# A fixed deviation bound, proved at the end, and pair differences from one fp16 half on two 32-row products

## The chip, the cores and the metric

The kernel runs on one core of a Trainium2 chip. The time is device microseconds of one execution of the whole kernel, as the median of several runs. One execution was taken with the hardware profiler; its trace gives the start and length of each instruction on TensorE (PE, with PEld for its weight loads), VectorE (DVE), ScalarE (ACT), GpSimd (POOL) and SyncE (SP, which issues the DMAs).

## The reference

There are 4 batches of 12480 tokens with 128 channels, 32 inducing points, and an MLP of 2048 hidden units with a squared ReLU.

```python
def mab(q, kv):
    s = scale * (q @ kv.transpose(0, 2, 1))
    a = softmax(s)                      # over the last axis, +1e-09 in the sum
    return a @ kv
h = mab(I, x)                           # per batch: 32 rows of 128
attn = mab(x, h)                        # per token: 32 weights, then a @ h
r = np.maximum(attn @ w_in, 0.0)        # 2048 columns
out = (r * r) @ w_out                   # 128 columns
```

## The kernel before

A token's attention output is a mix of the 32 rows of h with weights a that lie close to 1/32. So the kernel writes a = 1/32 + d and multiplies h into w_in once per batch. A hidden column whose 32 values all have one sign under every possible d needs no ReLU: it is either dead or plainly squared. The squares of all plain columns together are a quadratic form in d, with 512 coefficients: 16 x 31 pair differences and 16 further rows. Columns of mixed sign are few (at most 16 are allowed) and are computed one by one. A bound rho on the deviation says which column is which.

For each batch b the program has four parts:

- `first(b)` (L240): scores of 7 groups G of tokens (`scores`, L234, four fp32 products side by side on 32 columns each), their exponentials, and h by `hacc` (L323). Inside it `largest(G)` (L290) takes, on DVE, the largest magnitude of each row of the group's x, 128 x 1920 values.
- `prepare(b)` (L437): h times w_in (`hwv`, L448), the bound rho from the largest x and the spread of h (L454 to L459, L474 to L485), the sorting of the columns (L499 to L513), and from these the weights `w16` (L605 to L613), `lin`, `osc` and `bias` of the quadratic form.
- `second(b, G)` (L349): the token scores against h, their softmax, and d = a - 1/32, scaled by 2^14, as an upper and a lower fp16 half (L385 to L388). Both go to DRAM (L389) and come back transposed by `load_dT` (L404): rows 0 to 31 of `dT` are the upper half, 32 to 63 the lower, 64 to 95 the upper again. `squares` (L414) fills rows 96 to 127 with the mixed columns.
- `Chunk` (L629), 26 of 480 tokens in each batch: `up(j)` for j = 0, 1 makes two products of `pairs` with dT into two PSUM banks (`hp`, L639); `lift(j)` squares both on ACT in one instruction (L648); `down()` multiplies by w16 (four products, L654) and lin (one, L655) and brings the result out with scale and bias on ACT (L658) or DVE (L660), and SP stores it (L661).

`up` gives its product 96 rows. The matrix `pairs` (L106 to L114) holds one difference of unit vectors per column, once on rows 0 to 31 and again on 32 to 63, so that upper and lower half are added.

The order of the work is written out in the loop at L739: lift, the next chunk's up, the chunk before's down, then `background` (L721), which gives out pieces of `second`, `squares`, and the next batch's `first` and `prepare` by fixed counts. A scheduler with its own estimates of instruction lengths then orders each engine's queue; instructions whose inputs are early can be put far ahead. `hp` has two buffers, so `up` waits for the `lift` of the chunk before. Where an operation can run on ACT or DVE, `to_act` (L152) compares the sums in `held`, to which the program adds what it gives each engine; `largest` adds about 2 us to DVE's each time (L291). At the end the flags of all batches (the bound was small enough, few enough mixed columns, sizes fit) pick whether the general path `every_column` has to run (L899); in these runs it does not.

Of the kernel before, what the change touches and what calls it, by code (L numbers as in the profile page):

```python
# [9 lines left out]
F32 = mybir.dt.float32  # L10
# [20 lines left out]
MX = 16  # L31
RHO_MAX = 2.0 ** -8
NX = 9
# [7 lines left out]
def attend_then_relu2_mlp(ctx: ExitStack, tc: tile.TileContext, xn, xT, indT, w_in, w_out, outT):  # L41
# [65 lines left out]
    nc.vector.memset(pairs, 0.0)  # L107
    fold_f = fold.rearrange("p k i -> p (k i)")
    for s in range(1, 17):
        n = MI if s < 16 else 16  # L110
        nc.vector.tensor_tensor(
            pairs[0:64, MI * (s - 1):MI * (s - 1) + n], fold_f[0:64, 0:n], fold_f[0:64, s:s + n], op=ALU.subtract,
        )
    nc.vector.tensor_copy(pairs[0:64, 31 * 16:32 * 16], fold_f[0:64, 0:16])  # L114

# [3 lines left out]
    inv_t = const.tile([P, 1], F32, name="inv_t")  # L119
    flags = const.tile([1, NB], F32, name="flags")  # L120

# [4 lines left out]
    for k in range(2):  # L126
        one = Batch()
        one.xm = const.tile([P, NG], F32, name=f"xm{k}")
# [111 lines left out]
    def first(b):  # L240
# [48 lines left out]

        def largest(G):  # L290
            held["dve"] += 60 + 1.042 * 4 * WID[G]  # L291
            nc.vector.tensor_reduce(  # L292
                st.xm[:, G:G + 1], st.xp[G], axis=AX.X, op=ALU.max, apply_absolute_value=True,
            )

        def exp(G):
# [10 lines left out]
        for G, nb32 in enumerate(BLK):  # L307
# [5 lines left out]
            if G + 2 < NG:  # L313
                exp(G + 2)
            largest(G)
            yield
# [32 lines left out]
    def second(b, G, again=False):  # L349
# [39 lines left out]
        nc.sync.dma_start(st.ad[:, :, :, 480 * G:480 * G + w].rearrange("q i h n -> (q i) h n"), a16[:, :, 0:w])  # L389
        if not again:  # L390
            st.aT[G] = load_dT(b, G)
        yield
# [44 lines left out]
    def prepare(b):  # L437
# [6 lines left out]
        for h in range(2):  # L444
            ps = att_psum(f"hwv_{b}_{h}")
            for k in range(8):
                f = (8 * h + k) * P
                nc.tensor.matmul(  # L448
                    ps[:, k * (MI + 1):(k + 1) * (MI + 1)], w_in_sb[:, f:f + P], st.hT[:, 96:P + 1], start=True, stop=True,
                )  # L450
            evac(hwv[:, 8 * h:8 * h + 8].rearrange("p k i -> p (k i)"), ps[:, 0:8 * (MI + 1)], 8 * (MI + 1))
            if h == 0:

                xm, dh, ah = small("xm"), small("dh", MI), small("ah", MI)  # L454
                nc.vector.tensor_reduce(xm, st.xm, axis=AX.X, op=ALU.max)
                ts(dh, st.hT[:, 0:MI], st.hT[:, P:P + 1], None, op0=ALU.subtract)
                stt(dh, dh, -1.0, dh, op0=ALU.mult, op1=ALU.max)
                stt(ah, st.hT[:, 0:MI], -1.0, st.hT[:, 0:MI], op0=ALU.mult, op1=ALU.max)
                stt(dh, ah, 2.0 ** -18, dh, op0=ALU.mult, op1=ALU.add)  # L459
            yield  # L460
# [12 lines left out]
        nc.tensor.transpose(ps[0:1, 0:P], am, ident)  # L473
        nc.tensor.matmul(ps[0:1, P:P + MI], xm, dh, start=True, stop=True)  # L474
        row = work.tile([1, 2], F32, tag="row", name=f"row_{b}")
        nc.vector.tensor_reduce(row[:, 0:1], ps[0:1, 0:P], axis=AX.X, op=ALU.max)
        nc.vector.tensor_reduce(row[:, 1:2], ps[0:1, P:P + MI], axis=AX.X, op=ALU.max)
        ts(row[:, 0:1], row[:, 0:1], 2.0 ** -60, None, op0=ALU.max)
        ts(row[:, 1:2], row[:, 1:2], 2 * scale * (1 + 2.0 ** -8), 2.0 ** -16, op0=ALU.mult, op1=ALU.add)
        yield  # L480
        ps = att_psum(f"bc_{b}")
        nc.tensor.matmul(ps[:, 0:2], ones, row, start=True, stop=True)
        two = small("two", 2)
        nc.vector.tensor_copy(two, ps[:, 0:2])
        rho = two[:, 1:2]  # L485
        p2 = small("p2")
        ts(p2.bitcast(I32), two[:, 0:1].bitcast(I32), 0x7F800000, None, op0=ALU.bitwise_and)
        mg, nmg, s, k2, omr = small("mg"), small("nmg"), small("s"), small("k2"), small("omr")
        ts(k2, p2, 2.0, None, op0=ALU.mult)
# [10 lines left out]
        ts(nmg, p2, -2.0 ** -16, None, op0=ALU.mult)  # L500
        ts(omr, rho, -1.0, 1.0, op0=ALU.mult, op1=ALU.add)
# [7 lines left out]
        ts(dn, lo, 0.0, rho, op0=ALU.min, op1=ALU.mult)  # L509
        tt(dn, dn, vm, op=ALU.add)  # L510
# [34 lines left out]
        stt(inc, inc, pl, mix, op0=ALU.add, op1=ALU.mult)  # L545
        fits = work.tile([1, 2], F32, tag="fits", name=f"fits_{b}")
        ts(fits[:, 0:1], bp[0:1, 2:3], MX + 0.5, None, op0=ALU.is_le)
        ts(fits[:, 1:2], row[:, 1:2], RHO_MAX, None, op0=ALU.is_le)
        tt(flags[:, b:b + 1], fits[:, 0:1], fits[:, 1:2], op=ALU.mult)

# [78 lines left out]
    class Chunk:  # L629
# [73 lines left out]
    N_SECOND, N_SCORES, N_HEADS, N_PRE, N_SQ = 4, 2 * NG, 20, 23, 2  # L703
    ahead = chain(*(second(b, G) for b in range(NB) for G in range(NG)))
    sqs = chain(*(squares(b, G) for b in range(NB) for G in range(NG)))
# [15 lines left out]
    def background(k):  # L721

        b, c = k // (2 * NCH), k % (2 * NCH) / 2.0
        give("ahead", ahead, min(math.ceil((NG * b + c / 4 + min(3, 2 + k / 16)) * N_SECOND), NB * NG * N_SECOND))
        if b + 1 < NB:
# [214 lines left out]
```

## Time and profile before

| | us |
|---|---|
| median of 3 runs | 576.62 (575.87 to 576.66) |
| profiled execution, first to last instruction | 577.3 |
| PE busy | 438.9 |
| DVE busy | 365.3 |
| ACT busy | 296.8 |
| POOL busy | 83.4 |

The profiled execution's span is the whole time that the trace shows of it; it lies 0.7 us above the median. A busy PE is not a PE at its peak: the length of a matmul in the trace contains the way through the array, and consecutive ones overlap. So the distance from start to start is what counts there.

### The profile page before, as it was taken

The page shows a single profiled execution, that of the slowest core. Times are in us where ns is not written, and L with a number is a line of the kernel's source. Part 1 is how long each engine was busy: PE and PEld are TensorE (multiplying, and loading weights), DVE is VectorE, ACT ScalarE, POOL GpSimd, SP SyncE. Part 2 cuts the span into 40 slices and gives each one's busy share as a digit, 9 for nine tenths or more (in the row PEclk, how much of TensorE's full clock was granted, in tenths as well). Part 3 has the DMA queues.
Part 4 walks back from the last instruction along what each step waited for, and adds up shares of the span by engine and source line. Part 5 has one row for each costly group of instructions (what it writes and reads, how often), then busy time and mean ns, then how long its engine had stood idle before and what let it go on. Part 6 is the DMA issues. An engine that isn't in the chain of part 4 may idle for free.

```text
span 577.3 us, 8820 instructions
## 1 busy us (share of the span) xinstructions
PE 438.9 (76%) x3083; PEld 204.5 (35%) x3083; DVE 365.3 (63%) x947; ACT 296.8 (51%) x419; POOL 83.4 (14%) x93
## 2 busy tenths in 40 slices
PE   1615465777798889769878899769777999897882
PEld 0014334522233536413333545313243555223330
DVE  6999758662555268997254298985534378767342
ACT  0030112437577266747875376628574476565771
POOL 0000011030211010242021021222011022422010
PEclk9999655997789569989889799969969599899997
DMA  8958715024528606565867535735866332334543
GB/s 322 399 214 277 277 69 154 1 86 155 179 80 305 199 20 226 172 182 167 280 226 230 178 102 186 270 104 145 311 211 190 107 105 72 97 126 130 168 132 131
DMA packets 64590, 100.82 MB, mean 175 GB/s; under 512 B 22800, under 2 KB 53776, under 8 KB 64528
## 3 DMA queue, kind: packets, MB, share of 16 engines
q1 hardware_dynamic: 64528, 100.08, 52.1%
q8 instruction: 28, 0.46, 0.3%
q14 instruction: 34, 0.28, 0.2%
HBM read 64.91 MB, written 31.95 MB: 168 GB/s over the span
## 4 chain that ended last, share of the span: by engine, by line
PE 44%; DVE 28%; ACT 13%; issue 6%; DMA 3%; POOL 3%; SPq 1%; POOLq 0%; ACTq 0%; DVEq 0%
PE po L654 10%; PE hp L639 9%; ACT g L648 8%; PE s L236 7%; DVE xm L292 5%; PE hwv L448 5%; PE hacc L323 4%; DVE G L605 3%; DMA outT_dram<-o 2%; PE po L655 2%; PE wq L611 2%; ACT o L658 2%; DVE e L362 2%; PE R L529 2%; DVE z L372 2%
## 5 line engine op out<-in xcount | busy, mean ns | idle before, releaser
L648 ACT ACTIVATE g<-hp 128x960 f16<-128x960 f32 x208 | 193.2, 970 | 87.9 <-PE hp L639 48.9
L639 PE MATMUL hp<-dT,pairs 96*128 96x480 f16 x416 | 122.0, 385 | 29.0 <-ACT g L648 28.1
L654 PE MATMUL po<-g,w 128*128 128x480 f16 x416 | 119.4, 399 | 16.1 <-ACT o L658 6.0
L368 POOL TENSOR_TENSOR e<-e,mx 128x480 f32<-128x480 f32 (+1 forms) x28 | 26.5, 947 | 334.8 <-DVE mx L364 222.8
L639 PEld LDWEIGHTS <-pairs 96*128 96x128 f16 x416 | 37.8, 99 | 97.6 <-issue 75.7
L654 PEld LDWEIGHTS <-w 128*128 128x128 f16 x416 | 41.1, 104 | 75.4 <-issue 43.9
L292 DVE TENSOR_REDUCE xm<-xp_False 128x1 f32<-128x1920 f32 (+1 forms) x28 | 55.7, 1989 | 5.3 <-DMA xp_False<-xT_dram 5.3
L658 ACT ACTIVATE o<-po,bias,osc 128x480 f32<-128x480 f32 x66 | 48.9, 753 | 18.9 <-PE po L655 7.1
L236 PE MATMUL s<-xp_False,indT_sb 128*32 128x480 f32 (+1 forms) x224 | 37.7, 743 | 20.5 <-DMA xp_False<-xT_dram 12.3
L323 PE MATMUL hacc<-xnb,en 128*32 128x128 f32 x784 | 39.2, 328 | 17.2 <-issue 9.3
L655 PE MATMUL po<-dT,lin 128*128 128x480 f16 x104 | 42.3, 408 | 2.7 <-DMA dT<-zz 2.7
L432 POOL TENSOR_TENSOR zz<-z 128x480 f16<-128x480 f32 (+1 forms) x28 | 28.9, 1030 | 87.8 <-DVE z L428 72.1
L660 DVE TENSOR_SCALAR o<-po,osc,bias 128x480 f32<-128x480 f32 x38 | 28.7, 767 | 18.0 <-DMA outT_dram<-o 6.8
L323 PEld LDWEIGHTS hacc<-xnb,en 128*32 128x32 f32 x784 | 26.7, 129 | 34.3 <-issue 20.1
L300 ACT ACTIVATE sT<-sT,nb 128x480 f32<-128x480 f32 (+1 forms) x28 | 18.2, 653 | 35.5 <-DVE nb L287 35.5
L236 PE MATMUL s<-xp_False,hT 128*32 128x480 f32 (+1 forms) x224 | 34.5, 628 | 2.1 <-DVE s L357 1.7
L375 POOL TENSOR_TENSOR e<-e,z 128x480 f32<-128x480 f32 (+1 forms) x28 | 27.6, 986 | 53.8 <-DVE z L374 48.6
L428 DVE TENSOR_SCALAR z<-sq,off,cut 128x480 f32<-128x480 f32 (+1 forms) x28 | 21.4, 764 | 21.8 <-PE sq L422 21.7
L605 DVE TENSOR_TENSOR G<-hwp,hw 128x512 f16<-128x512 f16 x64 | 30.1, 510 | 5.0 <-PE wq L611 4.7
L369 ACT ACTIVATE e<-e 128x480 f32<-128x480 f32 (+1 forms) x28 | 16.1, 574 | 31.6 <-POOL e L368 31.6
L362 DVE STREAM_TRANSPOSE e<-s 128x480 f32<-128x480 f32 (+1 forms) x28 | 18.0, 644 | 15.4 <-PE s L236 14.9
L331 DVE TENSOR_TENSOR hq<-hacc,hq 128x128 f32<-128x128 f32 x24 | 6.8, 284 | 33.0 <-PE hacc L323 33.0
(208 smaller groups left out, 498.6 us busy)
## 6 DMA issues: line engine op xcount, KB each, us to landing
outT_dram<-o SPq DMA_DIRECT2D x104, 240.0 KB, 2.2
xp_False<-xT_dram SPq DMA_DIRECT2D x24, 960.0 KB, 5.8
xnb<-xn_dram SPq DMA_DIRECT2D x28, 448.0 KB, 6.1
xnb<-xn_dram SPq DMA_DIRECT2D x24, 512.0 KB, 5.8
dT<-ad SPq DMA_DIRECT2D x72, 120.0 KB, 2.7
ad<-a SPq DMA_DIRECT2D x24, 240.0 KB, 2.7
dT<-zz SPq DMA_DIRECT2D x104, 30.0 KB, 1.9
wi<-w_in_dram SPq DMA_DIRECT2D x4, 512.0 KB, 5.4
```

Source lines behind the costliest of these rows:

```text
L236: nc.tensor.matmul(ps[32 * q:32 * q + 32, 0:w], lhsT, xp[:, w * q:w * q + w], start=True, stop=True,)
L292: nc.vector.tensor_reduce(st.xm[:, G:G + 1], st.xp[G], axis=AX.X, op=ALU.max, apply_absolute_value=True,)
L323: st.last = nc.tensor.matmul(hacc[32 * q:32 * q + 32, 0:P], en[:, t], xg[:, t % 8], start=t < 4, stop=t + 4 >= nb32,)
L362: nc.vector.transpose(ef[:, 0:wb], ps[:, 0:wb])
L432: nc.gpsimd.tensor_tensor(g[rows], zv[rows], zv[rows], op=ALU.mult)
L448: nc.tensor.matmul(ps[:, k * (MI + 1):(k + 1) * (MI + 1)], w_in_sb[:, f:f + P], st.hT[:, 96:P + 1], start=True, stop=True,)
L605: tt(g[:, :, MI * j:MI * j + n], hwp[:, :, 0:n], hw16f[:, :, s0:s0 + n], op=ALU.mult)
L639: nc.tensor.matmul(hp[:, i, 0:CH].rearrange("p (q t) -> p q t", q=4), pairs[0:96, (2 * j + i) * P:(2 * j + i + 1) * P], self.dT[0:96], sta ...
L648: nc.scalar.activation(self.g[:, 2 * j:2 * j + 2], self.hp.pop(j)[:, 0:2, 0:CH], AF.Square)
L654: nc.tensor.matmul(po[:, 0:CH], st.w16[:, i], self.g[:, i], start=i == 0, stop=False)
L655: nc.tensor.matmul(po[:, 0:CH].rearrange("p (q t) -> p q t", q=4), st.lin, self.dT, start=False, stop=True)
L658: nc.scalar.activation(o, po[:, 0:CH], AF.Identity, bias=st.bias, scale=st.osc)
```

## The change

- `largest` and everything that made rho from data goes: the 28 reductions over x, the spread of h, one small product, and the second column of `row`, `two` and `fits`. rho is the constant 2^-10.
- `second` gains one DVE instruction for each group: the elementwise minimum of the upper half of d with a running minimum `least_d` (128 x 480 fp16). After the last group `smallest()` reduces it, and one more flag says whether every d was at least -0.498, which is what rho = 2^-10 asks for.
- `pairs` has each difference once: for products with even number on rows 0 to 31, for odd ones on rows 64 to 95. `up(j)` multiplies the first product with rows 0 to 31 of dT and the second with rows 64 to 95, so each has 32 rows, and the lower half of d (rows 32 to 63) is not used there. `squares` and `lin` read dT as before.

```diff
-RHO_MAX = 2.0 ** -8
+RHO = 2.0 ** -10
+D_MIN = -0.498
...
+    def half_rows(block):
+        return slice(64, 96) if block % 2 else slice(0, 32)
+
     for s in range(1, 17):
         n = MI if s < 16 else 16
+        r = half_rows((s - 1) // 4)
         nc.vector.tensor_tensor(
-            pairs[0:64, MI * (s - 1):MI * (s - 1) + n], fold_f[0:64, 0:n], fold_f[0:64, s:s + n], op=ALU.subtract,
+            pairs[r, MI * (s - 1):MI * (s - 1) + n], fold_f[r, 0:n], fold_f[r, s:s + n], op=ALU.subtract,
         )
...
+    least_d = const.tile([P, CH], F16, name="least_d")
+    nc.vector.memset(least_d, 0.0)
...
-        def largest(G):
-            held["dve"] += 60 + 1.042 * 4 * WID[G]
-            nc.vector.tensor_reduce(
-                st.xm[:, G:G + 1], st.xp[G], axis=AX.X, op=ALU.max, apply_absolute_value=True,
-            )
...
-            largest(G)
...
         if not again:
+            nc.vector.tensor_tensor(least_d[:, 0:w], least_d[:, 0:w], a16[:, 0, 0:w], op=ALU.min)
             st.aT[G] = load_dT(b, G)
...
-            if h == 0:
-
-                xm, dh, ah = small("xm"), small("dh", MI), small("ah", MI)
-                nc.vector.tensor_reduce(xm, st.xm, axis=AX.X, op=ALU.max)
...
-        nc.tensor.matmul(ps[0:1, P:P + MI], xm, dh, start=True, stop=True)
...
-        ts(vm, v, omr, None, op0=ALU.mult)
-        ts(up, hi, 0.0, rho, op0=ALU.max, op1=ALU.mult)
+        ts(vm, v, 1.0 - RHO, None, op0=ALU.mult)
+        ts(up, hi, 0.0, RHO, op0=ALU.max, op1=ALU.mult)
...
             for i in range(2):
+                r = half_rows(i)
                 nc.tensor.matmul(
-                    hp[:, i, 0:CH].rearrange("p (q t) -> p q t", q=4), pairs[0:96, (2 * j + i) * P:(2 * j + i + 1) * P],
-                    self.dT[0:96], start=True, stop=True,
+                    hp[:, i, 0:CH].rearrange("p (q t) -> p q t", q=4), pairs[r, (2 * j + i) * P:(2 * j + i + 1) * P],
+                    self.dT[r], start=True, stop=True,
                 )
...
+    def smallest():
+
+        m = small("dmin")
+        nc.vector.tensor_reduce(m, least_d, axis=AX.X, op=ALU.min)
+        tp = att_psum("dmin_t")
+        nc.tensor.transpose(tp[0:1, 0:P], m, ident)
+        t = work.tile([1, 1], F32, tag="dmin1", name="dmin1")
+        nc.vector.tensor_reduce(t, tp[0:1, 0:P], axis=AX.X, op=ALU.min)
+        nc.vector.tensor_scalar(flags[:, NB:NB + 1], t, D_MIN, None, op0=ALU.is_ge)
+        yield
```

## Rows read from the trace of the kernel before

**Rows 1.** The page: engines' busy time, and the granted TensorE clock in 40 slices.

```profile
PE 438.9 (76%) x3083; PEld 204.5 (35%) x3083; DVE 365.3 (63%) x947; ACT 296.8 (51%) x419; POOL 83.4 (14%) x93
PEclk9999655997789569989889799969969599899997
```

**Rows 2.** Busy time by stretch: PE, PEld, DVE, ACT, POOL, then clock, DMA share, GB/s.

```profile
12.00:62.50 50.50, 24.10 (x255) 11.22 (x255) 49.16 (x93) 4.66 (x14) 0.00 (x0) 0.98 0.83 306
69.50:93.20 23.70, 11.82 (x55) 8.05 (x55) 15.68 (x54) 5.65 (x9) 4.42 (x4) 0.50 0.30 100
...
107.00:507.00 400.00, 336.52 (x2414) 153.94 (x2411) 244.35 (x651) 239.81 (x344) 66.59 (x68) 0.87 0.52 166
507.00:569.00 62.00, 51.18 (x241) 19.91 (x240) 33.38 (x55) 39.43 (x45) 11.23 (x12) 0.99 0.46 148
```

**Rows 3.** The chain that ended last, in order of time: start, us, what; L292 alone.

```profile
13.21 2.06 DVE xm L292
...
64.95 2.06 DVE xm L292
83.18 2.06 DVE xm L292
251.44 2.01 DVE xm L292
...
379.35 2.06 DVE xm L292
```

**Rows 4.** The page: that chain, by line.

```profile
PE po L654 10%; PE hp L639 9%; ACT g L648 8%; PE s L236 7%; DVE xm L292 5%; PE hwv L448 5%; PE hacc L323 4%; DVE G L605 3%; DMA outT_dram<-o 2%; PE po L655 2%; PE wq L611 2%; ACT o L658 2%; DVE e L362 2%; PE R L529 2%; DVE z L372 2%
```

**Rows 5.** Groups by line: shapes, count, busy us, mean ns, idle before by releaser.

```profile
L292 DVE TENSOR_REDUCE xm<-xp_False 128x1 f32<-128x1920 f32 (+1 forms) x28 | 55.7, 1989 | 5.3 <-DMA xp_False<-xT_dram 5.3
L648 ACT ACTIVATE g<-hp 128x960 f16<-128x960 f32 x208 | 193.2, 970 | 87.9 <-PE hp L639 48.9 <-PE po L654 32.5 <-DMA dT<-ad 5.8
L639 PE MATMUL hp<-dT,pairs 96*128 96x480 f16 x416 | 122.0, 385 | 29.0 <-ACT g L648 28.1
L660 DVE TENSOR_SCALAR o<-po,osc,bias 128x480 f32<-128x480 f32 x38 | 28.7, 767 | 18.0 <-DMA outT_dram<-o 6.8 <-ACT g L648 5.8 <-PE po L655 2.8
L605 DVE TENSOR_TENSOR G<-hwp,hw 128x512 f16<-128x512 f16 x60 | 29.3, 525 | 5.0 <-PE wq L611 4.7
L504 DVE TENSOR_SCALAR vm<-hwv,omr 128x16 f32<-128x16 f32 x4 | 1.6, 393 | 0.0
```

**Rows 6.** PE in order of time: the first and the last visit to L639.

```profile
99.65 0.98 PE L639 MATMUL hp<-dT,pairs 96*128 96x480 f16 x4
...
563.62 0.57 PE L639 MATMUL hp<-dT,pairs 96*128 96x480 f16 x2
```

**Rows 7.** PE in order of time: products of one shape, and changes between shapes.

```profile
546.58 0.98 PE L639 MATMUL hp<-dT,pairs 96*128 96x480 f16 x4
537.70 0.56 PE L639 MATMUL hp<-dT,pairs 96*128 96x480 f16 x2 [0.40 <-ACT g L648]
538.20 0.39 PE L422 MATMUL sq<-dT,singles 96*32 96x480 f16 x4
538.57 0.56 PE L639 MATMUL hp<-dT,pairs 96*128 96x480 f16 x2
476.16 0.58 PE L639 MATMUL hp<-dT,pairs 96*128 96x480 f16 x2
476.67 0.51 PE L578 MATMUL cat<-cat,rep 32*96 32x160 f32 x2
```

**Rows 8.** PE in order of time, before and after the clock falls at 282.5 us.

```profile
280.41 0.56 PE L639 MATMUL hp<-dT,pairs 96*128 96x480 f16 x2 [0.41 <-ACT g L648]
283.00 0.96 PE L639 MATMUL hp<-dT,pairs 96*128 96x480 f16 x2 [0.26 <-ACT g L648]
```

More of the change, by code (lines that the diff above doesn't have):

```diff
@@ L108, in attend_then_relu2_mlp @@
     fold_f = fold.rearrange("p k i -> p (k i)")
+    def half_rows(block):
+        return slice(64, 96) if block % 2 else slice(0, 32)
     for s in range(1, 17):
         n = MI if s < 16 else 16
+        r = half_rows((s - 1) // 4)
         nc.vector.tensor_tensor(
-            pairs[0:64, MI * (s - 1):MI * (s - 1) + n], fold_f[0:64, 0:n], fold_f[0:64, s:s + n], op=ALU.subtract,
+            pairs[r, MI * (s - 1):MI * (s - 1) + n], fold_f[r, 0:n], fold_f[r, s:s + n], op=ALU.subtract,
         )
-    nc.vector.tensor_copy(pairs[0:64, 31 * 16:32 * 16], fold_f[0:64, 0:16])
+    r = half_rows(NQ - 1)
+    nc.vector.tensor_copy(pairs[r, 31 * 16:32 * 16], fold_f[r, 0:16])
     w_in_sb = const.tile([P, NF * P], F32, name="w_in_sb")
@@ L119, in attend_then_relu2_mlp @@
     inv_t = const.tile([P, 1], F32, name="inv_t")
-    flags = const.tile([1, NB], F32, name="flags")
+    flags = const.tile([1, NB + 1], F32, name="flags")
+    least_d = const.tile([P, CH], F16, name="least_d")
+    nc.vector.memset(least_d, 0.0)
     class Batch:
@@ L127, in attend_then_relu2_mlp @@
         one = Batch()
-        one.xm = const.tile([P, NG], F32, name=f"xm{k}")
         one.hn = const.tile([P, P], F32, name=f"hn{k}")
@@ L451, in prepare @@
             evac(hwv[:, 8 * h:8 * h + 8].rearrange("p k i -> p (k i)"), ps[:, 0:8 * (MI + 1)], 8 * (MI + 1))
-            if h == 0:
-                xm, dh, ah = small("xm"), small("dh", MI), small("ah", MI)
-                nc.vector.tensor_reduce(xm, st.xm, axis=AX.X, op=ALU.max)
[L456 to L459, printed above, removed]
             yield
@@ L473, in prepare @@
         nc.tensor.transpose(ps[0:1, 0:P], am, ident)
-        nc.tensor.matmul(ps[0:1, P:P + MI], xm, dh, start=True, stop=True)
[L475 to L479, printed above, removed]
+        row = work.tile([1, 1], F32, tag="row", name=f"row_{b}")
+        nc.vector.tensor_reduce(row, ps[0:1, 0:P], axis=AX.X, op=ALU.max)
+        ts(row, row, 2.0 ** -60, None, op0=ALU.max)
         yield
         ps = att_psum(f"bc_{b}")
[L482 to L485, printed above, removed]
+        nc.tensor.matmul(ps[:, 0:1], ones, row, start=True, stop=True)
         p2 = small("p2")
-        ts(p2.bitcast(I32), two[:, 0:1].bitcast(I32), 0x7F800000, None, op0=ALU.bitwise_and)
-        mg, nmg, s, k2, omr = small("mg"), small("nmg"), small("s"), small("k2"), small("omr")
+        ts(p2.bitcast(I32), ps[:, 0:1].bitcast(I32), 0x7F800000, None, op0=ALU.bitwise_and)
+        mg, nmg, s, k2 = small("mg"), small("nmg"), small("s"), small("k2")
         ts(k2, p2, 2.0, None, op0=ALU.mult)
@@ L500, in prepare @@
         ts(nmg, p2, -2.0 ** -16, None, op0=ALU.mult)
-        ts(omr, rho, -1.0, 1.0, op0=ALU.mult, op1=ALU.add)
         up, dn, dead, pos, mix, inc = (small(n, NF) for n in ("up_c", "dn_c", "dead", "pos", "mix", "inc"))
         vm = small("vm", NF)
-        ts(vm, v, omr, None, op0=ALU.mult)
-        ts(up, hi, 0.0, rho, op0=ALU.max, op1=ALU.mult)
+        ts(vm, v, 1.0 - RHO, None, op0=ALU.mult)
+        ts(up, hi, 0.0, RHO, op0=ALU.max, op1=ALU.mult)
         tt(up, up, vm, op=ALU.add)
@@ L508, in prepare @@
         stt(dead, up, nmg, dead, op0=ALU.is_le, op1=ALU.max)
-        ts(dn, lo, 0.0, rho, op0=ALU.min, op1=ALU.mult)
+        ts(dn, lo, 0.0, RHO, op0=ALU.min, op1=ALU.mult)
         tt(dn, dn, vm, op=ALU.add)
@@ L545, in prepare @@
         stt(inc, inc, pl, mix, op0=ALU.add, op1=ALU.mult)
[L546 to L549, printed above, removed]
+        ts(flags[:, b:b + 1], bp[0:1, 2:3], MX + 0.5, None, op0=ALU.is_le)
         hot = flow.tile([P, NF, MX], F32, tag="hot", name=f"hot_{b}", bufs=1)
@@ L703, in attend_then_relu2_mlp @@
     N_SECOND, N_SCORES, N_HEADS, N_PRE, N_SQ = 4, 2 * NG, 20, 23, 2
-    ahead = chain(*(second(b, G) for b in range(NB) for G in range(NG)))
+    def smallest():
[7 more added lines that the diff above has]
+        yield
+    ahead = chain(*(second(b, G) for b in range(NB) for G in range(NG)), smallest())
     sqs = chain(*(squares(b, G) for b in range(NB) for G in range(NG)))
@@ L723, in background @@
         b, c = k // (2 * NCH), k % (2 * NCH) / 2.0
-        give("ahead", ahead, min(math.ceil((NG * b + c / 4 + min(3, 2 + k / 16)) * N_SECOND), NB * NG * N_SECOND))
+        give("ahead", ahead, min(math.ceil((NG * b + c / 4 + min(3, 2 + k / 16)) * N_SECOND), NB * NG * N_SECOND + 1))
         if b + 1 < NB:
```

## The prediction, made before the changed kernel was run

> **What bounds the kernel now.** I read the busy shares first, then the stretches, then the chain. The shares [rows 1] name PE, 76% busy, with DVE at 63% and ACT at 51%, but they are averages over two different stages. The stretches [rows 2] part them. From 12 to 62.5 us, in `first(0)` and the unpacking of the weights, DVE is busy 49.2 of 50.5 us and PE 24.1: this is a DVE stage, with the DMA queues not far behind at a share of 0.83. From 107 to 507 us, in the chunks with the next batch's work between them, PE is busy 337 of 400 us, DVE 244, ACT 240: a PE stage, and its granted clock is 0.87, so about a quarter of it ran at the lower of the two levels, 1.2 instead of 2.4 GHz. From 507 to 569 us only chunks and the last `second` groups are left; PE 51 of 62, ACT 39, DVE 33: nobody is full, the engines wait for each other. The chain by line [rows 4] says the same: five of the seven largest shares are PE's matmuls of the chunks and of the batch work, and the largest DVE line in it is L292, the reduction over x, with 5% (29 us). In order of time [rows 3] it stands there in 13 pieces, nearly all of 2.06 us: eight before 84 us, five between 251 and 382.
>
> **Removing the reductions.** L292 costs 28 x 1.99 = 55.7 us of DVE [rows 5]. Only what lies on the chain can come back.
>
> Six of the eight early pieces lie before 62.5 us, 6 x 2.06 = 12.4 us of a full DVE. Next in line there are the loads: the DMA share of 0.83 means that the same bytes at a share of 1 take 0.83 x 50.5 = 41.9 us, so at most 8.6 us come back if all of them are needed, and all 12.4 if the loads for batch 1 among them can land later. I take 10.5 us. The seventh piece, at 64.95, stands between the two steps of one reciprocal: it belongs to batch 1 and was put ahead by the scheduler, as was the one just before it. Together they hold up h for about 3.3 us, which nothing covers. The eighth (83.18) holds `prepare(0)` for 2.06 us; I count 2.0. That is 15.8 us ahead of the chunks.
>
> The five later pieces make 9.5 us on the chain. PE waits there for `second` and `first`, which also run through POOL and ACT, and those are late next: I count 6.5, between 2 and 9.5. PE also stood idle there long enough for its clock to fall afterwards; I add 2 us for matmuls that keep the higher level (0 to 4).
>
> **Short instructions.** Each `prepare` loses some fourteen short DVE instructions and a product of 32 columns. The longest that changes takes 0.39 us (L504) [rows 5]; most are far shorter and lie beside other work in the later batches. In batch 0 a few of them are on the chain: 0.5 us.
>
> **The running minimum.** 28 fp16 instructions of 128 x 480. The nearest row is L605, fp16 by fp16 to fp16, 128 x 512 in 525 ns [rows 5]: 28 x 0.49 = 14 us of DVE. They stand after the store of d is issued, so the store doesn't wait; what waits is the next DVE instruction. In the PE stage DVE has 156 us to spare and the cost is nothing; if that cover is gone at a batch's start, where the `second` groups crowd, two or three of them show. I count 1.3 us (0 to 6). `smallest()` runs some chunks before the end, ahead of stores that are later, and costs nothing; its flag only adds one value to the last reduction.
>
> **The balance of ACT and DVE.** The reductions of batches 1 to 3 no longer add to `held`, some 40 us in all. Moving one output from ACT to DVE closes the gap by about 1.2 us, so some 33 outputs move. DVE takes 0.77 us for one [rows 5], which gives back 25 of the 56 us that it lost; ACT sheds about as much. DVE comes to about 365 - 56 - 8 + 14 + 25 = 340 us, under PE. I count nothing, within 5 us either way.
>
> **The two products side by side.** This is the disputed part. Products of one shape start every 0.20 us at the higher clock: two of L639 end 0.56 us after the first start, four 0.98 [rows 7]. No row shows two groups of rows at work at once. The nearest is L422, where four products on four groups of 32 columns take 0.39 us together, as long as one: full overlap. The other end is no overlap. I take full overlap, since the pairs go to separate rows of the array and separate PSUM banks as those go to separate columns.
>
> But a change of shape isn't free. In the same rows the second L639 starts at 537.90, the L422 group at 538.20 and the next L639 at 538.57: 0.30 and 0.37 us where 0.20 is usual, so 0.10 to enter and 0.17 to leave. Entering a product of 32 rows costs the same: L639 at 476.16 and 476.36, L578 at 476.67, 0.31 us. So a lone pair costs 0.20 + 0.10 + 0.17 = 0.47 us as a visit to another shape, where two products now take 0.40.
>
> The Trainium skill, "TensorEngine Tiling (Array Packing)", section Key Properties, says it outright: changing the tiling mode, not merely the tile, drains the engine. The trace agrees, with 0.10 to 0.17 us for each change. Its page "TensorE: Matmul & The Clock Gate", section Measured speedup vs the span model, has four row tiles at 3.07 times; no run here shows that yet.
>
> So what counts is how often the work comes to L639. In PE's order of time there are 143 unbroken visits between the first and the last [rows 6]: 64 of two products, 35 of four, 16 of one, 15 of three, 13 longer. They hold 191 pairs: 191 x 0.20 = 38 us saved. 54 visits come from another shape already (scores, hacc, squares) and 52 go to one; there nothing is added. That leaves 89 entries at 0.10 and 91 exits at 0.10 to 0.17, 21 us, less 2.5 for the 25 visits that begin after an idle stretch. Net 20 us of PE at the higher clock, some 5 more where it is at the lower, since a pair takes 0.40 us longer there (0.96 against 0.56) [rows 8]. L639's share on the chain is 9%, 49 us, against 416 x 0.20 = 83 us of it in all and more where the clock is low: about half. I count 11 us, between a loss of 9 (no overlap, the changes paid, half on the chain) and a gain of 25 (all).
>
> **Sum.** 15.8 + 6.5 + 2 + 0.5 - 1.3 + 11 = 34.5 us, from a span of 577.3 to 542.8. The median lies 0.7 lower than that span: 542.
>
> **Rivals.** (a) The pairs give nothing, because they don't overlap or the changes eat it. For it: a lone pair, the commonest visit, costs 0.47 against 0.40 by the rows. Against: 48 of the visits hold four or more. Then early 15.5, later 4, and hp between 0 and -9: 557 to 566, say 560.
>
> (b) PE limits throughout 107 to 507 us, so all of its saving counts, and the loads don't hold the start back. For it: 337 of 400 us busy. Against: only half of L639 is on the chain, and two `hp` buffers still tie PE to ACT, whose lifts take 208 x 0.97 = 202 us [rows 5]. 17.5 + 9.5 + 4 + 25 = 56 less 1: 521 to 526.
>
> (c) Slower: the clock. At 280 to 282 us PE did nothing but pairs, each after a wait of 0.3 to 0.4 us for ACT, and just afterwards the same pair took 0.96 instead of 0.56 us [rows 8]: sparse pairs lost it the higher level. Overlapped pairs are sparser still. A chunk's seven product slots (two pairs, five others) take 1.4 us more at the lower level; where PE limits, 25 chunks more of the 104 at that level eat the 34.5 us, and beyond that it is slower, at 50 chunks some 610. Against: at the lower level PE is fuller, and got the higher one back each time so far.
>
> (d) The change doesn't do what it says: a flag fails and the general path runs. Worked out from the reference's inputs the least scaled d is about -0.064, far from -0.498. I give it nothing.
>
> **How the numbers follow.** My forecast, 532 to 553: 0.57. (a) 0.21, (b) 0.15, (c) 0.05, and 0.02 for mishaps that end at no change. The range takes in the forecast and most of (a) and (b): 521 to 562. About 0.2%, 1.2 us, is what a measurement of this kernel can tell from no change. Faster 0.94, same 0.02, slower 0.04 (part of (c) still ends faster).
>
> **What would show it.** The first lift after the tiles of batch 0 should come some 15 us earlier. If DVE from 12 to 50 us still is full, or PE waits there for xn loads, the first term is off. In PE's order two L639 of a pair should start a few ns apart (overlap) or 0.20 us apart (none), and the product after a pair 0.3 us or more after it. The granted clock from the first chunk to the end should stay near 0.87; below 0.75 means (c). DVE's total should be near 340 us and ACT's near 272; if DVE waits appear before `down`'s outputs, the balance was not free. The prediction is wrong if the scheduler, with DVE's 56 us gone, orders the queues so differently that PE waits in new places; the chain by line would then show a new name.

## The result, and the profile after

The changed kernel takes 566.4 us as the median of four runs (559.3, 563.7, 569.1, 571.7), beside 576.6 for the kernel before on the same chip (575.9 to 577.8). That is a gain of 10 us where 34.5 were forecast, and the time lies above the range. The ratio is 0.972 with an interval of 0.966 to 0.978 from its two faster executions, which alone are compared, here and in every ratio below; by the medians of all four it is 0.982. Even by the former the gain is 16 us, less than half of the forecast. Inside the four the time goes with the mean granted clock: 0.840, 0.819, 0.797 and 0.801 in the order of the times. In the kernel before that clock differs as much, from 0.83 to 0.91, and the times (575 to 583 us over all its runs) show no order by it; so it isn't the mean alone that counts.

The page of the kernel after: the busy line and the clock line answer to [rows 1], and the groups by line that follow to [rows 5].

```profile
PE 426.6 (77%) x3076; PEld 188.1 (34%) x3076; DVE 336.8 (60%) x941; ACT 273.4 (49%) x385; POOL 84.2 (15%) x93
PEclk9996559987995789799595889799696998877777
L633 ACT ACTIVATE g<-hp 128x960 f16<-128x960 f32 x208 | 191.8, 970 | 109.5 <-PE hp L624 69.0
L639 PE MATMUL po<-g,w 128*128 128x480 f16 x416 | 129.7, 426 | 15.1 <-ACT o L643 6.8
L624 PE MATMUL hp<-dT,pairs 32*128 32x480 f16 x416 | 89.3, 394 | 39.3 <-ACT g L633 38.9
L645 DVE TENSOR_SCALAR o<-po,osc,bias 128x480 f32<-128x480 f32 x64 | 48.4, 767 | 18.1 <-PE po L640 11.5
L643 ACT ACTIVATE o<-po,bias,osc 128x480 f32<-128x480 f32 x40 | 29.4, 755 | 9.8 <-ACT g L633 3.0
```

The totals came as forecast: DVE 336.8 us (340), ACT 273.4 (272), and the pairs (now L624) 89.3 us instead of 122.0. But PE's total fell by 12 us only. And the clock line has five sevens at its end, where the line of before has four nines and one seven.

The stretches of the kernel after: PE, PEld, DVE, ACT and POOL busy, clock, DMA share, GB/s. The four are the first stage, `hwv` to the first lift, the first product of `lin` to the first one of the last batch, and the last batch from its first product of `lin` to its last. Behind them that last stretch in the kernel before, 67.8 us.

```profile
12.00:49.50 37.50, 19.50 (x192) 8.08 (x188) 35.48 (x86) 4.66 (x14) 0.00 (x0) 0.93 0.94 349
56.90:86.80 29.90, 19.48 (x128) 14.03 (x127) 18.84 (x67) 7.02 (x12) 4.15 (x4) 0.60 0.49 164
110.30:468.90 358.60, 298.93 (x2260) 134.15 (x2260) 214.84 (x609) 206.71 (x295) 62.74 (x63) 0.86 0.55 180
468.90:545.90 77.00, 63.11 (x256) 18.78 (x256) 39.71 (x74) 42.77 (x49) 13.20 (x15) 0.78 0.40 127
...
499.30:567.10 67.80, 56.78 (x255) 21.28 (x255) 38.79 (x68) 43.09 (x50) 14.24 (x15) 0.95 0.44 142
```

With the same points in the trace of before (the first product of `lin` at 127.6 us, the last batch's first at 499.3, its last at 567.1, the end at 577.3) the two profiled executions come apart like this: the start is 17.3 us shorter (110.3 against 127.6), the three batches up to the last are 13.1 shorter (358.6 against 371.7), the last batch 9.2 longer (77.0 against 67.8), the end 1.4 longer. Together 19.8 us, 577.3 to 557.5. The profiled execution is the one of 559.3 us; the others, 4 to 12 us longer, had a lower mean clock, and where they lost the time no trace shows.

So in this execution the start brought what was forecast and a little more, and the last batch took back half of it: the same 256 products, 77.0 us instead of 67.8, at a clock of 0.78 instead of 0.95, although half of the products of `up` no longer take time of their own.

That they take none is seen in PE's order of time (start, length, line, and idle time before).

```profile
508.92 0.37 PE L640 MATMUL po<-dT,lin 128*128 128x480 f16 x1
509.22 0.58 PE L624 MATMUL hp<-dT,pairs 32*128 32x480 f16 x4
509.73 0.98 PE L639 MATMUL po<-g,w 128*128 128x480 f16 x4
510.55 0.37 PE L640 MATMUL po<-dT,lin 128*128 128x480 f16 x1
510.85 0.38 PE L624 MATMUL hp<-dT,pairs 32*128 32x480 f16 x2
511.52 0.38 PE L624 MATMUL hp<-dT,pairs 32*128 32x480 f16 x2 [0.29 <-ACT g L633]
...
516.20 1.36 PE L639 MATMUL po<-g,w 128*128 128x480 f16 x3 [1.47 <-DVE o L645]
```

A pair takes 0.38 us, as long as one product; its two products start 2 to 6 ns apart. The first pair begins 0.30 us after the product before it, where 0.20 is usual, and L639 begins 0.51 us after the first of two pairs, which is 0.20 from pair to pair and 0.30 or so to leave. A lone pair as a visit takes 0.20 + 0.10 + 0.10 = 0.40 us: as much as two products of 96 rows one after the other. The last line is from the lower level: three products in 1.36 us, where four take 0.98 above.

### The profile page after: what moved, and what is told of

The parts are those of the page before. It is cut to its first block, busy times and chain, and to the rows that moved or that the text cites. A ratio compares the mean times of both kernels' runs of the same rounds, so it can differ in the third digit from the quotient of the medians.

```text
span 557.5 us, 8743 instructions
## 1 busy us (share of the span) xinstructions
PE 426.6 (77%) x3076; PEld 188.1 (34%) x3076; DVE 336.8 (60%) x941; ACT 273.4 (49%) x385; POOL 84.2 (15%) x93
## 5 line engine op out<-in xcount | busy, mean ns | idle before, releaser
L639 PE MATMUL po<-g,w 128*128 128x480 f16 x416 | 129.7, 426 | 15.1 <-ACT o L643 6.8
L624 PE MATMUL hp<-dT,pairs 32*128 32x480 f16 x416 | 89.3, 394 | 39.3 <-ACT g L633 38.9
L639 PEld LDWEIGHTS <-w 128*128 128x128 f16 x416 | 38.7, 108 | 86.0 <-issue 69.1
L645 DVE TENSOR_SCALAR o<-po,osc,bias 128x480 f32<-128x480 f32 x64 | 48.4, 767 | 18.1 <-PE po L640 11.5
L624 PEld LDWEIGHTS <-pairs 32*128 32x128 f16 x416 | 21.8, 92 | 108.6 <-issue 107.0
L244 PE MATMUL s<-xp_False,indT_sb 128*32 128x480 f32 (+1 forms) x224 | 34.8, 696 | 17.9 <-DMA xp_False<-xT_dram 11.9
L643 ACT ACTIVATE o<-po,bias,osc 128x480 f32<-128x480 f32 x40 | 29.4, 755 | 9.8 <-ACT g L633 3.0
L589 DVE TENSOR_TENSOR G<-hwp,hw 128x512 f16<-128x512 f16 x64 | 27.3, 461 | 7.8 <-PE wq L595 7.7
L171 ACT COPY hwv<-hwv 128x264 f32<-128x264 f32 x8 | 3.0, 379 | 55.3 <-PE hwv L450 55.3
L379 DVE STREAM_TRANSPOSE a<-e 128x480 f32<-128x480 f32 (+1 forms) x28 | 17.9, 641 | 18.9 <-POOL e L376 18.9
L262 DVE TENSOR_SCALAR_CACHE_REDUCE sT<-s 128x480 f32<-128x480 f32 (+1 forms) x28 | 17.3, 619 | 19.5 <-PE s L244 19.2
```

Of the source, the lines that this page charges most:

```text
L244: nc.tensor.matmul(ps[32 * q:32 * q + 32, 0:w], lhsT, xp[:, w * q:w * q + w], start=True, stop=True,)
L589: tt(g[:, :, MI * j:MI * j + n], hwp[:, :, 0:n], hw16f[:, :, s0:s0 + n], op=ALU.mult)
L624: nc.tensor.matmul(hp[:, i, 0:CH].rearrange("p (q t) -> p q t", q=4), pairs[r, (2 * j + i) * P:(2 * j + i + 1) * P], self.dT[r], start=Tru ...
L639: nc.tensor.matmul(po[:, 0:CH], st.w16[:, i], self.g[:, i], start=i == 0, stop=False)
L643: nc.scalar.activation(o, po[:, 0:CH], AF.Identity, bias=st.bias, scale=st.osc)
L645: nc.vector.tensor_scalar(o, po[:, 0:CH], st.osc, st.bias, op0=ALU.mult, op1=ALU.add)
```

## The experiments

All times are medians, with the lowest and the highest run. The time at the lower level is worked out from an execution's mean granted clock c and its span as 2 x (1 - c) x span, since a clock of 1 is the upper and 0.5 the lower level. The experiments ran in four groups, each on another chip; the kernel before, beside each group, took 577.3 to 578.0 us.

| kernel | products of `up` | outputs (ACT/DVE) | us | clock of executions |
|---|---|---|---|---|
| before | 96 rows | 66/38 | 577 (575 to 583) | 0.83 to 0.91 |
| after | 32, side by side | 40/64 | 566.4 (559.3 to 571.7) | 0.80 to 0.84 |
| e1 | 96 | 40/64 | 564.0 (554.8 to 569.6) | 0.85 to 0.89 |
| e8 | 96 | 66/38 | 562.7 (559.8 to 567.0) | 0.87 to 0.89 |
| e5 | 32, side by side | 66/38 | 579.9 (575.5 to 582.4) | 0.79 to 0.83 |
| e2 (old bound) | 32, side by side | 66/38 | 585.2 (580.9 to 592.8) | 0.79 to 0.88 |
| e9 | 64, in turn | 40/64 | 573.3 (571.8 to 576.6) | 0.82 to 0.85 |
| e3 | 32, in turn | 40/64 | 593.0 (590.7 to 604.0) | 0.78 to 0.81 |
| e4 | 32; last batch 96 | 40/64 | 554.8 (553.0 to 559.8) | 0.83 to 0.87 |
| e10 | 32; first and last 96 | 40/64 | 556.7 (549.8 to 559.9) | 0.84 to 0.87 |

Two cautions for all of them. The scheduler orders each engine's queue anew for each kernel: in the traces of e9 and e3, which differ in a number of rows alone, 185 of PE's 3076 places hold another product. Differences of a few us between two kernels may be that order.

And the mean clock of an execution takes in the start, where PE isn't the limit. From 20 to 40 us, long before the first pair product (83 us or later), it shows either level, first the kernel after, then e3:

```profile
20.00:40.00 20.00, 9.90 (x95) 4.08 (x87) 18.16 (x45) 4.66 (x14) 0.00 (x0) 1.00 0.97 349
...
20.00:40.00 20.00, 9.99 (x95) 4.18 (x87) 18.16 (x45) 4.66 (x14) 0.00 (x0) 0.50 0.96 347
```

Up to the first pair product the kernel after and e1 spent 34 us at the lower level, e3, e9, e5 and e6 61, and `hwv` begins between 56.3 and 56.9 us in all six. So for the profiled executions the clock over the chunks says more, from the first product of `lin` to the last.

### The two halves of the change, each alone

**e1** is the kernel after with the old products of 96 rows, **e2** the kernel before with the new pairs.

```diff
 # e1, against after
     def half_rows(block):
-        return slice(64, 96) if block % 2 else slice(0, 32)
+        return slice(0, 64)
...
-                    hp[...], pairs[r, (2 * j + i) * P:(2 * j + i + 1) * P],
-                    self.dT[r], start=True, stop=True,
+                    hp[...], pairs[0:96, (2 * j + i) * P:(2 * j + i + 1) * P],
+                    self.dT[0:96], start=True, stop=True,
```

> The fixed bound and the running minimum as in the changed kernel, but the pair products as before: 96 rows, upper and lower half, one after the other. Theory 'clock' (the overlapped pairs leave PE sparser, and the lower clock level takes back what they save): the start of batch 0 as in the changed kernel (hwv at 57 us instead of 69.5), granted clock 0.86 or more, 552 to 560 us, executions within 2 us of each other. Rival 'shape' (the changes of tile shape eat the pairs' gain, the clock is a side effect): about the same time, 555 to 563, but with the clock near the changed kernel's 0.84.

> The kernel before, with the pair products alone changed: 32 rows each, side by side. Both theories: start unchanged (hwv near 69.5 us). 'Clock': granted clock 0.80 to 0.85, the last batch longer than its 68 us of before, 572 to 584 us, executions spread by several us. 'Shape': clock near 0.87, 566 to 575 us, little spread.

Measured: e1 564.0 us (ratio 0.976, 0.965 to 0.987), not to be told from the whole change. e2 585.2 us in ten runs, 8 us slower than before (1.012, 1.007 to 1.016). So the bound made the whole gain, and the pairs, which were to bring 11 us more, brought none. e1 lies 4 us above the range of 'clock', with executions 15 us apart instead of 2, and e2 1 us above it. The lines of e1, PE's total and its three costliest groups of the chunks, against those of the kernel after:

```profile
PE 425.5 (77%) x3076; PEld 201.7 (36%) x3076; DVE 337.1 (61%) x941; ACT 273.3 (49%) x385; POOL 84.2 (15%) x93
PEclk9996559989997899899897999899696899697997
L623 PE MATMUL hp<-dT,pairs 96*128 96x480 f16 x416 | 121.3, 380 | 33.4 <-ACT g L632 31.6 <-DMA outT_dram<-o 0.7
L638 PE MATMUL po<-g,w 128*128 128x480 f16 x416 | 117.2, 391 | 16.6 <-ACT o L642 7.2 <-DVE o L644 6.8 <-ACT g L632 1.3
L639 PE MATMUL po<-dT,lin 128*128 128x480 f16 x104 | 40.9, 398 | 6.5 <-DMA dT<-zz 6.5
```

The pairs save 32 us at their own line (121.3 to 89.3), and PE's total is the same, 425.5 and 426.6. The clock line ends in 9697997 where the other ends in 8877777. Of what came back, 12.5 us stand at the products by w16, which nobody touched: 391 ns each here, 426 in the kernel after. That is the clock alone: within the higher level one takes some 367 ns in both traces, within the lower some 600, and 97 of the 416 lie within the lower in the kernel after, 42 in e1.

### Rows and overlap, parted

**e3** puts both products on rows 0 to 31, so that they can't lie side by side; **e9** gives each product rows 0 to 63. Both have the changes of shape, neither the overlap.

```diff
     def half_rows(block):
-        return slice(64, 96) if block % 2 else slice(0, 32)
+        return slice(0, 32)     # e3;  slice(0, 64) in e9
```

> The changed kernel with both products of a pair on rows 0 to 31 of the array: 32 rows each and all changes of shape kept, but no overlap, so PE streams as long as before. 'Clock': the lower level is rarer than in the changed kernel (0.86 or more, last batch at the higher level), so the 38 us of lost overlap cost little: 560 to 570 us with small spread. 'Shape': clock as in the changed kernel, and about half of the 38 us on the chain: 578 to 590 us.

> As the run with one row group, but 64 rows each (upper and lower half of d on rows 0 to 63, the old matrix): again no overlap and a change of shape at each visit; only the height of the product differs. Theory 'height' (the clock falls with 32-row products): granted clock 0.84 or more, low level under 190 us, 575 to 583 us. Theory 'changes' (the stops at changes of shape cost it the clock): clock as with 32 rows on one group, 0.78 to 0.81, 588 to 600 us.

Measured: e9 573.3 us (0.992, 0.989 to 0.995), e3 593.0 (1.025, 1.015 to 1.034). Neither theory's range holds e3's time; e9 is on the side of 'height', 2 us under its range. The clock and the products of `up` in both, e9 first; then the chunks from the first product of `lin` to the last in e1, e9, e3 and the kernel after:

```profile
core 0: 574.8 us, clock 0.822
L624 PE MATMUL hp<-dT,pairs 64*128 64x480 f16 x416 | 126.7, 396 | 27.8 <-ACT g L633 26.7 <-DMA outT_dram<-o 0.7
...
core 0: 590.3 us, clock 0.779
L624 PE MATMUL hp<-dT,pairs 32*128 32x480 f16 x416 | 130.4, 407 | 27.5 <-ACT g L633 26.3 <-DMA dT<-ad 0.6
...
110.30:542.30 432.00, 360.28 (x2517) 165.50 (x2516) 255.06 (x682) 249.39 (x344) 75.95 (x77) 0.91 0.53 171
117.70:563.50 445.80, 386.52 (x2516) 158.47 (x2516) 253.73 (x683) 250.70 (x344) 76.32 (x77) 0.86 0.51 166
118.60:578.80 460.20, 407.25 (x2516) 165.54 (x2516) 254.23 (x683) 250.66 (x344) 76.13 (x77) 0.81 0.50 161
110.30:545.90 435.60, 362.04 (x2516) 152.93 (x2516) 254.55 (x683) 249.49 (x344) 75.95 (x77) 0.84 0.53 170
```

From 96 over 64 to 32 rows, each product taking its own time: 564, 573, 593 us, and the clock over the chunks falls with it, 0.91, 0.86, 0.81. Side by side on 32 rows it is 566 us, at 0.84. So the overlap is real and worth 27 us (593.0 - 566.4), each kernel at the clock that it got, and the narrow product costs as much: 9 us to 64 rows (the changes of shape among them) and 20 more to 32. My idea up to here was that the clock fell because PE has less to do when pairs overlap. e3 speaks against it: there each product takes its own time as in e1, and the clock is lower still than with pairs side by side, 0.78 over the whole execution, where I had expected 0.86 or more. (PE's busy time is the longest there too, 480.5 us, but partly because the lower clock makes it longer.)

### Where the clock costs: the last batch

**e4** gives the last batch alone products of 96 rows, with a second matrix `pairs96` as in the kernel before. **e10** does so for the first batch too. **e6** keeps the pairs and makes each of the last batch's twice, over the same bank, which changes no value.

```diff
 # e4 (e10: self.b in (0, NB - 1))
             for i in range(2):
-                r = half_rows(i)
+                whole = self.b == NB - 1
+                r = slice(0, 96) if whole else half_rows(i)
...
-                    hp[...], pairs[r, (2 * j + i) * P:(2 * j + i + 1) * P],
+                    hp[...], (pairs96 if whole else pairs)[r, (2 * j + i) * P:(2 * j + i + 1) * P],
 # e6
-            for i in range(2):
+            for i in (0, 1, 0, 1) if self.b == NB - 1 else (0, 1):
```

> The changed kernel with 96-row products one after the other in the last batch alone (a second matrix, built on GpSimd beside the start). 'Clock': from the first store of the last batch to its last product 66 to 70 us instead of 77, granted clock there above 0.93, total 547 to 555 us. 'Shape': the last batch also shorter by its changes of shape, some 5 us, but its clock stays near 0.8; total 553 to 562 us.

> The changed kernel with each pair product of the last batch issued twice into the same place: 10 us of PE work more, of no use, all changes of shape kept. 'Clock': the last batch (first to last product of lin) falls from 77 to 69 to 73 us, at a granted clock above 0.9, total below the changed kernel's 566 by 3 to 8 us. 'Shape': last batch 77 us or more, total 566 to 574.

> The changed kernel with 96-row products one after the other in batches 0 and 3, overlapped pairs in 1 and 2 alone. If the pairs only pay where PE is full, that is in batches 1 and 2: 548 to 553 us. If batch 0 profits too, 555 to 560.

Measured: e4 554.8 us (0.961, 0.953 to 0.970), e6 561.0 (0.970, 0.964 to 0.975), e10 556.7 (0.958, 0.951 to 0.965). By their medians e4 and e10 are faster than both kernels. The last batch from its first product of `lin` to its last, in e4, e6 and e3:

```profile
473.00:542.70 69.70, 57.98 (x256) 21.72 (x256) 40.67 (x74) 42.46 (x49) 13.34 (x15) 0.93 0.43 138
...
478.10:549.50 71.40, 63.10 (x336) 19.78 (x336) 38.16 (x68) 42.76 (x48) 11.42 (x13) 0.87 0.41 135
...
496.50:578.80 82.30, 70.62 (x256) 21.22 (x256) 40.18 (x74) 43.18 (x49) 13.38 (x15) 0.75 0.37 120
```

With 96 rows the stretch takes 69.7 us at a clock of 0.93, 7.3 less than in the kernel after, as 'clock' expected. In e6 PE gets 336 products instead of 256, none of the additional ones of any use, and the stretch takes 71.4 us instead of 77.0. More work in less time can't come from the work; the clock is 0.87 instead of 0.78 (above 0.9 was expected), that is 19 us at the lower level instead of 34. PE's order in e4 is that of the kernel after for the first 2823 products, just into the last batch, and in e6 for the first 2733, so up to there the order of the queue is not the cause. But it is one execution of each, and as a whole e6 can't be told from the kernel after: the ratios are 0.970 and 0.972, and in its profiled execution the stretch begins 9.2 us later. Over the profiled executions of all the kernels this holds: the last batches with 96 rows throughout take 66 to 71 us with 7 to 16 us at the lower level, those with 32 or 64 rows 73 to 82 with 27 to 41.

Ahead of the last batch it is not so plain. e10's first batch, with 96 rows, takes 119 us to the next batch's first product of `lin`, e4's with pairs 116, and the ranges of their times overlap: there the pairs neither help nor hurt visibly, though 556.7 lies in the range that was put down for a profit in batch 0.

### The balance of ACT and DVE

**e5** is the kernel after, but `held` gets what it got for the reductions, so that as many outputs go to ACT as before. **e8** is the same with 96 rows, **e7** the same with 96 rows in the last batch alone. **e11** puts all outputs on DVE.

```diff
 # e5; also in e7, e8
                 exp(G + 2)
+            held["dve"] += 60 + 1.042 * 4 * WID[G]
             yield
 # e11
-            if to_act(220 + 0.833 * CH, 110 + 1.042 * CH):
+            held["dve"] += 110 + 1.042 * CH
+            if False:
```

> The changed kernel with the old balance: DVE is still credited with the 2 us per reduction that it no longer does, so as many outputs go to ACT as before (66, not 40). Theory 'shift' (outputs on DVE stand behind the softmax work in its queue and hold PE's next product): 555 to 561 us, PE waits less for DVE outputs. Theory 'clock alone': the shift is free, within 3 us of the changed kernel's 566.

> The fixed bound alone with 96-row products and the old balance of ACT and DVE: only the reductions go and the running minimum comes. 'Shift': 553 to 558 us, batches 2 and 3 no longer than in the kernel before (123 and 121 us), spread under 6 us. 'Clock alone': about 564 as with the new balance.

> The kernel with 96-row products in the last batch alone, with the old balance of ACT and DVE. 'Shift': 546 to 551 us, under the 554.8 without it. 'Clock alone': 553 to 557.

> The changed kernel with all 104 outputs of the chunks on DVE. If the pairs need a free ACT (moving 32 outputs to DVE was worth 13.5 us with pairs, nothing with 96 rows): 552 to 561 us. If that was the order of the queues and not the load: 566 or more, as DVE takes 31 us more.

Measured: e5 579.9 us in ten runs (1.003, 1.000 to 1.006), e8 562.7 (0.972, 0.965 to 0.979), e7 575.9 in ten runs (0.986, 0.981 to 0.991), e11 593.9 (1.026, 1.021 to 1.031). PE's total and PE's groups of the chunks in e8, then in e5:

```profile
PE 433.2 (77%) x3076; PEld 205.1 (36%) x3076; DVE 320.3 (57%) x907; ACT 295.4 (52%) x419; POOL 84.9 (15%) x93
L624 PE MATMUL hp<-dT,pairs 96*128 96x480 f16 x416 | 121.5, 384 | 34.8 <-ACT g L633 34.0
L639 PE MATMUL po<-g,w 128*128 128x480 f16 x416 | 118.9, 397 | 16.2 <-DVE o L645 9.1 <-ACT o L643 2.8 <-ACT g L633 2.7
...
PE 443.8 (76%) x3076; PEld 194.4 (33%) x3076; DVE 320.0 (55%) x907; ACT 296.2 (51%) x419; POOL 83.7 (14%) x93
L625 PE MATMUL hp<-dT,pairs 32*128 32x480 f16 x416 | 91.5, 403 | 46.5 <-ACT g L634 42.1
L640 PE MATMUL po<-g,w 128*128 128x480 f16 x416 | 132.4, 437 | 15.0 <-DVE o L646 7.8 <-ACT o L644 5.4 <-ACT w L173 0.8
```

With the old balance the pairs cost 17 us (562.7 to 579.9), the two ranges far apart. They save 30 us at their own line, and PE's total still rises by 10.6: at the same 208 lifts and 104 outputs, each product by w16 takes 437 ns instead of 397. With the new balance the pairs cost 2.4 us, within the spread.

How much of that lies in the last batch e7 doesn't settle: by the medians 96 rows there bring 4 of the 17 us back (579.9 to 575.9), by the ratios (1.003 and 0.986) 10, and its ten runs spread from 567 to 583. In the profiled executions of e5 and e8 4.5 us lie between the last batch's first and last product of `lin` (72.9 and 68.4 us), and 10.3 in the three batches before it.

Neither theory's range holds e5 or e7; e8 came out as 'clock alone' said.

So the balance is worth nothing with 96 rows (564.0 and 562.7) and 13.5 us with pairs (566.4 and 579.9). That it isn't simply better to load DVE more is what e11 shows: all outputs there, and 593.9 us, on the side of the order and not of a free ACT. In the profiled executions the chunks of e5 spent 164 us at the lower level, those of the kernel after 137, of e8 92 and of e1 79, so the clock has a part in it again; but that is one execution of each, e5's of 582.4 us and the kernel after's of 559.3, at the far ends of their ranges. Why the two interact isn't settled: the kernels also differ in the order of PE's queue, and no run holds that order fixed while the balance moves.

### The reductions and the minimum

**e12** is e8 without the running minimum; **e13** is e8 with the reductions over x of batches 1 to 3 back in their place, 21 instructions.

```diff
 # e12
-            nc.vector.tensor_tensor(least_d[:, 0:w], least_d[:, 0:w], a16[:, 0, 0:w], op=ALU.min)
 # e13
+            if b:
+                nc.vector.tensor_reduce(
+                    xm_all[:, NG * b + G:NG * b + G + 1], st.xp[G], axis=AX.X, op=ALU.max, apply_absolute_value=True,
+                )
```

> The fixed bound with 96-row products and the old balance, without the running minimum (so nothing proves the bound; least_d stays zero). Compared with the same kernel with it, 562.7 us. Theory 'minimum in the way' (its 28 instructions took back what the reductions gave in batches 1 and 2): 554 to 559 us, batches 2 and 3 no longer than before (123 and 121 us). Theory 'hidden': 560 to 565, the minimum is free and the reductions of the later batches were free as well.

> The fixed bound with 96-row products and the old balance, with the 21 reductions of batches 1 to 3 back in their places (results not used). Compared with the same kernel without them, 562.7 us. Theory 'on the chain' (8.5 us as forecast): 568 to 574 us, of which 5 from the three that the scheduler puts before 84 us. Theory 'hidden in the chunks': 563 to 568 us, all of the change's gain is in the start.

Measured: e12 559.2 us (556.6 to 569.3), e13 564.8 (560.3 to 569.2), e8 between them with 562.7 (559.8 to 567.0). Their groups, the minimum from the kernel after and the reductions from e13:

```profile
L392 DVE TENSOR_TENSOR least_d<-least_d,a 128x480 f16<-128x480 f16 (+1 forms) x28 | 11.1, 397 | 0.0
...
L321 DVE TENSOR_REDUCE xm_all<-xp_False 128x1 f32<-128x1920 f32 (+1 forms) x21 | 41.7, 1986 | 9.7 <-DMA xp_False<-xT_dram 9.7
```

41.7 us of DVE put back cost some 2 us, and 11.1 us taken away bring some 3.5; neither can be told from nothing with runs that spread over 7 to 13 us. e13 came out as 'hidden in the chunks', e12 between its two theories.

Hidden doesn't mean that nothing waits for a reduction. What PE waited for, in e13 and then in e8 (us in all, times, the longest):

```profile
PE sq L431 <- DVE xm_all L321: 7.0, 2, 4.6
...
PE s L244 <- DVE z L431: 9.5, 2, 5.6
```

In e13 the 4.6 us end at 363.7 us, at the start of batch 2. In e8, without the reductions, PE stands idle early in the same batch, for 5.6 us up to 367.0, now for another DVE instruction.

## Why the prediction was wrong, point by point

**The start was right in its size, in part by luck.** Forecast 15.8 us from the reductions, 15 net with the first batch's other small terms. `hwv` begins at 56.9 us instead of 69.5, 12.6 earlier; the first lift comes 13.5 and the first product of `lin` 17.3 us earlier. In e1, e8 and e13 `hwv` begins within 0.6 us of the same place. But the forecast gave 3.3 of the 15.8 to two reductions of batch 1 that held up h. In e13 those are back, the first at 56.5 us, and `hwv` begins at 56.3 all the same: batch 0's reductions alone, counted at 10.5 us, brought the whole 13. And the first product of `lin` comes between 109.9 and 118.6 us in the kernels with the fixed bound, so the 17.3 are the good end of 9 to 18. What was to be late next is: the DMA share in the first stage is 0.94 where it was 0.83 [rows 2], at 349 GB/s.

**The later reductions: forecast 6.5 us and 2 for the clock, measured about 2 in all** (e13 against e8, although e13 puts the early ones of batch 1 back too). The step that failed took the five pieces of L292 on the chain after 250 us [rows 3] for gain, cut by a third. They were on the chain of one execution; with them gone a wait can end in another DVE instruction instead, as e8 shows early in batch 2. DVE has room there (214.8 of 358.6 us busy after the change), so they fit in again nearly free of cost.

**The minimum: forecast 14 us of DVE and 1.3 on the path**, measured 11.1 and at most a few. The price from the nearest row was too high by a quarter: 397 ns instead of 490.

**The balance: forecast 33 outputs and nothing in time.** 26 outputs moved, 64 on DVE instead of 38 [rows 5], and with them six of the upper halves `a16` from ACT to DVE, 32 in all. It cost nothing with 96 rows and is worth 13.5 us with pairs; "nothing, within 5" was right for the kernel in which I should have asked it and wrong for the one that I forecast.

**The pairs: forecast 11 us gained; measured nothing with the new balance (2.4 lost by the medians, 1.8 gained by the ratios), 8 and 17 lost with the old.** By e1 the bound with the new balance came out 10 us short of its part of the sum (13.3 us for 23.5), and the pairs 13 short; these make up the 24 that are missing. The steps one by one:

- Full overlap was right, and its size on PE too: 41 us at the line of `up` between e3 and the kernel after (130.4 to 89.3), where 38 were counted.
- The change of shape was right at the higher level, 0.10 us to enter and 0.10 to leave, the low end of the 0.10 to 0.17 put down for it. (Of the 91 exits that were priced, some 26 led into idle time in the trace of before, which the sum took off for the entries alone.) At the lower level a pair enters 0.54 us after the product before it and the next product follows after 0.51 to 0.53, where 0.40 is usual: the price grows with everything else.
- The visits are more numerous than in the kernel before: 155 instead of 143, 73 of two products and 22 of one. A lone pair gains nothing.
- The step that failed is the last: to price the saved PE time at the clock of the kernel before. "Some 5 more where it is at the lower" treated the level as given, while the change moved it. From the first product of `lin` to the last the profiled kernel after spent 137 of 436 us at the lower level, e1 79 of 432. PE was busy in 120 of the one and 71 of the other, so 49 us more of its work went at half the speed: by my estimate a loss of some 24 us. At the higher level the pairs save 208 x 0.20 = 42 us, and the 62 entries and 68 exits between `up` and the products by w16 and `lin` without idle time between, at 0.10 to 0.14 each, cost some 13. Those 29 us are more than the net 20 of the forecast; the clock took 24 of them, and 5 are left.

So rival (a), "the changes eat it", and rival (c), the clock, came together: neither alone is what happened. The time came out just above (a)'s, 557 to 566; the strength at which (c) turns the sign, 25 more chunks at the lower level, some 105 us at 4.2 us for a chunk, was not reached by the 58 more. In (c) I gave as the reason that overlapped pairs make PE sparser. That reason is refuted as it stands by e3, with the fullest PE and a clock lower still. What the runs show is narrower: less height of the products at the same spacing went with a lower clock over the chunks (96, 64, 32 rows: 0.91, 0.86, 0.81), useless products on top of the pairs went with a higher one (e6), and the last batch pays for it. What the chip looks at when it grants a level stays open, as does why the pairs cost 17 us with one balance and 2 with the other.

The Trainium skill was cited for one rule, in "TensorEngine Tiling (Array Packing)", section Key Properties: that changing the tiling mode drains the array. The traces agree, with 0.10 us each way. The figure cited from the Trainium skill, "TensorE: Matmul & The Clock Gate", section Measured speedup vs the span model, 3.07 times for four row tiles, is not shown by a run here; two of them ran in the time of one.

**What the profile was to show.** The list at the prediction's end named the right signs: the first lift 15 us earlier (13.5), two products a few ns apart (2 to 6), DVE and ACT at 340 and 272 (336.8 and 273.4). Its bound for the clock was "near 0.87", and "below 0.75 means (c)". The clock over the chunks was 0.86 up to the last batch and 0.78 in it: in between, where I had put nothing.

## What to carry to other kernels

A saving in TensorE time is priced at the clock that the changed kernel gets, not at that of the kernel before: here products of fewer rows came with a lower one, and every other product paid for it. Test such a part alone, and stage by stage: e4, which undoes it in the stage where it hurts, is by its median faster than either kernel. And a piece on the chain of one execution is a bound on what its removal brings, with the next wait just behind it; 42 us put back on an engine that isn't full cost about two.

## What the runs showed of the hardware

- Two products of 32 rows on separate rows of the array and separate banks start 2 to 6 ns apart and take 0.38 us together, as one does.
- A change to products of 32 rows costs 0.10 us and back again 0.10 at the higher level, at the lower level 0.14 and 0.11 to 0.13.
- At the same spacing, 416 products of 96, 64 or 32 rows among some 2660 others went with granted clocks of 0.91, 0.86 and 0.81 over the chunks of the profiled executions, and 564, 573 and 593 us as medians.
- A product of 480 columns by w16 took 366 to 368 ns on the mean within the higher level and 597 to 603 within the lower, in the traces of eight kernels.
- Work that nobody needs went with a shorter stretch: 80 more products in the last batch, 71.4 us instead of 77.0, at 0.87 instead of 0.78, in one execution of each.
- The granted clock of the start, the same work in each, was 1.00 in some executions and 0.50 in others (20 to 40 us), and `hwv` began between 56.3 and 56.9 us in six of them that were compared.
- Executions of the kernel after differ with the clock, 559 us at 0.840, 569 to 572 near 0.80; those of e8 (0.87 to 0.89) and of the kernel before show no such order.
